# A share of the exponentials on VectorE, taken from the fourth chunk of each batch instead of the third

## The chip, the cores and the metric

The kernel runs on one core of a Trainium2 chip. The metric is device time in microseconds (us). Before the change the median of four runs is 318.1 us (317.76, 320.7, 318.44 and 317.64 us). A program with its instruction order fixed by hand runs on five engines that only meet at semaphores: TensorE (PE in the profile, with its weight loads as PEld), VectorE (DVE), ScalarE (ACT), GpSimd (POOL) and the engine that issues most DMAs (SP).

## The reference

Attention with a soft cap for 8 batches of 12 heads, 448 positions and head size 64, followed by a soft mixture of experts (8 experts with 4 slots each, so 32 slots):

```python
scores = scale * q @ k^T                  # scale = 1/8
scores = cap * tanh(scores / cap)         # cap = 30
attn   = softmax(scores);  x = attn @ v   # x: 3584 x 768
logits = x @ phi                          # 3584 x 32
d = softmax over the tokens; slots = d^T @ x
slot_out[e] = relu(slots[e] @ w1[e]) @ w2[e]
out = softmax over the slots (logits) @ slot_out      # 3584 x 768
```

Since the scores are capped at 30, the kernel takes their exponentials without subtracting the maximum. Every score goes through one tanh and one exponential.

## The kernel before, in words

**Tiles.** Two heads make a pair, and two pairs a quad, whose q and k are loaded, cast and transposed together. A pair has 7 score tiles of 128 x 448 (64 keys of each of its two heads on the partitions, 448 queries along the row). The 336 tiles of the 48 pairs are cut into 56 chunks of 6 tiles without regard to where a pair ends. One batch is 42 tiles, that is 7 chunks, so the work repeats every 7 chunks, and what is told below by "chunk number modulo 7" holds for every batch.

**One pass of the main loop** (line 523) handles one chunk j and puts work on the engines in this order:

- ScalarE: tanh of the two halves of chunk j (line 278, 1344 elements per partition each, from PSUM to the bf16 tile `ex`), then the exponentials of the chunk before, j-1, in place (line 282, 2688 elements).
- TensorE: half 0 of the attention output of one pair ("pv", lines 314 to 322: 14 matmuls whose weights are the exponentials), the scores of the first half of chunk j+1 (line 269, six matmuls of 64x64), half 1 of the same pair's output, and the scores of the second half of chunk j+1. The pair is the one whose last tile lies in chunk j-2; in the passes with j modulo 7 equal to 2 there is none.
- VectorE: after each half of a pair, the norm: the reciprocal of the row sums (line 328) and the product with it (line 329), which frees the PSUM tile for the next half.

Score tiles have two buffers of three tiles each (`psS`), so TensorE may fill one only when ScalarE's tanh of two groups ago has read it. All of the pairs' outputs share one PSUM tile (`psV`, line 312), and all small products (transposes, logits, slot sums) share another (`psT`). The chunks of exponentials have four buffers.

**The slots.** Between these steps stand five places in each pass, "0", "a", "b", "c" and "d" in that order, at which a list written by hand (`aux`, lines 426 to 493) inserts further jobs: casts of the raw q and k on VectorE, their transposes on TensorE, filling matmuls ("junk", line 506) and the logits and slot sums. "a" follows half 0 of the pair and its norm, "c" follows half 1 and its norm, "d" ends the pass. Each engine runs its own instructions strictly in this order.

**The shared exponentials.** From the second batch on, one tile per batch, the first of one chunk, doesn't get its exponential from ScalarE but from VectorE (`poly_exp`, lines 291 to 304): seven instructions on 448 elements per partition, in three parts. Part 0 (lines 294, 296 and 298) turns the scaled score into the bits of a float and splits them into exponent `xe` and mantissa `xm`. Part 1 (lines 300, 301) and part 2 (lines 303, 304) evaluate a polynomial, and line 304 writes the result over the tanh in `ex`. For that chunk ScalarE's instruction is 2240 elements long and not 2688 (line 285). The list `shared` (line 289) holds chunks 9, 16, 23, 30, 37, 44 and 51, those with number modulo 7 equal to 2. Part 0 stands in "c" of the chunk's own pass, part 1 in "a" and part 2 in "c" of the next one.

In pass j modulo 7 = 2 there are also the cast of q in "c" (line 226), the transposes of q (line 237) with their copy (line 239) and the logits of a quad (lines 355 and 360) in "d". The logits' PSUM tile is the one that the transposes of q need next, so TensorE goes on when VectorE has read the logits (`lg`, line 360). At the start of pass j modulo 7 = 4 ScalarE takes the exponentials of a batch's logits (`e_exp`, line 366) and GpSimd copies them four times over (`e_rep`, line 372).

After the loop come the last pairs, the two layers of the experts, and the output, which is written by SP's DMAs.

Of the kernel before, what the change touches and what calls it, by code (L numbers as in the profile page):

```python
# [32 lines left out]
def kernel(  # L33
# [20 lines left out]
    cap = float(cap)  # L54
# [6 lines left out]
    NCH = NTILE // CH  # L61
# [224 lines left out]

    shared = [j for j in range(NCH - 2) if j % 7 == 2 and j > 7] if cap < 80 else []

    def poly_exp(j, part):
        t, bits = exs[j][:, 0, :], 2.0 ** 23
# [135 lines left out]
    def at(j, slot, f, *a):  # L428
        if j < 0:
            j, slot = 0, "b"  # L430
        aux.setdefault((j, slot), []).append((f, a))
# [16 lines left out]
    for b in range(B):  # L448
        j = b * PER
# [30 lines left out]
            if b % 2:  # L480
                at(j + 14, "d", e_sums, b // 2)
    for j in shared:
        for dj, slot, part in ((0, "c", 0), (1, "a", 1), (1, "c", 2)):
            at(j + dj, slot, poly_exp, j, part)
    for n, job in enumerate(wjobs):
        at(1 + n * (NCH - 5) // len(wjobs), "b", *job)
# [244 lines left out]
    for n in range(B // 2 * NT):  # L731
        bb, c = divmod(n, NT)
# [61 lines left out]
```

## Time and profile before

The profiled execution took 317.76 us; its span, from the first to the last instruction, is 316.0 us, at a mean granted TensorE clock of 0.987.

| | 7 to 100 us | 100 to 200 us | 200 to 269 us | 269 to 284 us | 284 to 316 us |
|---|---|---|---|---|---|
| ScalarE busy, us | 92.9 | 100.0 | 69.0 | 3.2 | 13.3 |
| TensorE matmuls busy, us | 82.6 | 89.7 | 62.2 | 14.5 | 14.8 |
| VectorE busy, us | 58.9 | 67.5 | 43.5 | 4.7 | 16.1 |
| GpSimd busy, us | 38.8 | 39.3 | 22.3 | 2.4 | 0.6 |
| DMA, GB/s | 240 | 233 | 209 | 325 | 351 |

The first three columns are the main loop, the fourth the end of the attention and the experts, the fifth the output. In a row of a group, "busy" is the sum of its instructions and the number behind the last bar is the time for which the engine stood still just before them, with what ended it. In a row of the timeline the first number is the start and the second the duration, and "[1.18 <-DVE lg L360]" means that the engine had been idle for 1.18 us until that instruction released it. The recorded durations of ScalarE's instructions overlap: the next one is started before the end of the one before. Their ends are regular: a chunk's end comes 4.69 to 4.70 us after that of the chunk before, 4.31 to 4.33 us where the chunk is a shared one.

### The profile page before, as it was taken

To read this page: it belongs to the slowest core of one execution; us is meant where nothing else is said; L and a number is where in the kernel's file an instruction comes from. 1 tells how busy PE (TensorE), PEld (TensorE's weight loads), DVE (VectorE), ACT (ScalarE), POOL (GpSimd) and SP (SyncE) were. 2 spreads that over 40 slices of the span, in tenths; PEclk is the share of its full clock that TensorE was granted. 3 is DMA by queue.
4 is the path that set the end of the run, shared out by engine and by line. 5 is a ranking of instruction groups with operands and counts; after the bars stand their busy time and mean duration, and the time that the engine had idled before them with its cause. 6 is when DMAs were issued, how large, how long until landed. Compare 5 with 4: busy or idle time off the path is not lost.

```text
span 316.0 us, 8844 instructions
## 1 busy us (share of the span) xinstructions
PE 269.3 (85%) x3804; PEld 189.6 (60%) x3804; DVE 193.3 (61%) x473; ACT 281.3 (89%) x208; POOL 105.5 (33%) x134
## 2 busy tenths in 40 slices
PE   8899897889789989898989988997989898998720
PEld 6667575666566656675666656765666577743300
DVE  3736665766676668666767586658665654337740
ACT  4999999999999999999999999999999999135730
POOL 2554341523542453354245415452543030200000
PEclk9999999999999999999999999999999999999995
DMA  8899999799999989999999999999999807798997
GB/s 232 268 228 241 291 249 263 170 226 256 213 225 244 255 222 222 232 235 280 174 250 257 235 224 207 253 233 249 214 240 230 213 14 228 250 399 298 389 413 310
DMA packets 57478, 77.68 MB, mean 246 GB/s; under 512 B 3808, under 2 KB 53600, under 8 KB 57440
## 3 DMA queue, kind: packets, MB, share of 16 engines
q0 software_dynamic: 30480, 25.22, 52.1%
q1 hardware_dynamic: 26672, 51.68, 47.6%
q8 instruction: 29, 0.48, 0.6%
q10 hardware_dynamic: 288, 0.23, 0.2%
q14 instruction: 9, 0.07, 0.1%
HBM read 91.32 MB, written 18.87 MB: 349 GB/s over the span
## 4 chain that ended last, share of the span: by engine, by line
ACT 51%; PE 30%; DVE 10%; DMA 2%; issue 2%; SPq 0%; DVEq 0%; ACTq 0%
ACT ex L278 26%; ACT ex L282 24%; PE pv L318 9%; PE sc L269 5%; PE junk L506 3%; PE so_ps L676 2%; DVE xq L329 2%; PE hp L649 2%; DMA out_dram<-ob 2%; PE kps L237 1%; PE xps L344 1%; PE op L702 1%; PE boot L506 1%; PE slps L407 1%; DVE xp L301 1%
## 5 line engine op out<-in xcount | busy, mean ns | idle before, releaser
L278 ACT ACTIVATE ex<-sc 128x1344 bf16<-128x1344 f32 (+1 forms) x113 | 159.3, 1652 | 0.9 <-PE sc L269 0.8
L282 ACT ACTIVATE ex<-ex 128x2688 bf16<-128x2688 bf16 (+4 forms) x58 | 156.2, 2698 | 0.1
L318 PEld LDWEIGHTS <-ex 128*128 128x128 bf16 x1344 | 78.7, 97 | 22.1 <-DVE xq L329 17.4
L318 PE MATMUL pv<-vbd,ex 128*128 128x130 bf16 x1274 | 89.5, 220 | 2.4 <-ACT ex L282 0.7
L269 PE MATMUL sc<-qT,kT 64*64 64x448 bf16 x672 | 78.6, 359 | 3.0 <-ACT ex L278 2.5
L247 POOL CAST vbd<-vraw 64x896 bf16<-64x896 f32 x23 | 21.4, 929 | 108.4 <-PE pv L318 70.5
L329 DVE TENSOR_TENSOR xq<-pv,rec 128x256 bf16<-128x256 f32 x91 | 38.6, 424 | 3.2
L328 DVE RECIPROCAL rec<-pv 128x4 f32<-128x4 f32 x91 | 16.6, 182 | 36.3 <-PE pv L318 36.3
L269 PEld LDWEIGHTS <-kT 64*64 64x64 bf16 x672 | 25.8, 105 | 20.7 <-issue 2.6
L506 PEld LDWEIGHTS <-ones 128*128 128x128 bf16 x470 | 28.6, 101 | 11.8 <-DVE xq L329 8.2
L506 PE MATMUL junk<-ones 128*128 128x128 bf16 x433 | 31.4, 219 | 2.7 <-DVE xq L329 1.9
L372 POOL COPY e<-E 128x512 bf16<-128x512 bf16 x9 | 5.9, 653 | 78.2 <-ACT E L366 46.3
L239 DVE COPY kT<-kps 128x896 bf16<-128x896 bf16 x23 | 14.4, 625 | 24.0 <-PE kps L237 23.9
L109 POOL DMA_DIRECT2D w1b<-in_moe_w_dram x32 | 25.2, 792 | 0.2 <-issue 0.2
L248 POOL CAST vbd<-vraw 64x896 bf16<-64x896 f32 x23 | 24.0, 1042 | 1.3
L346 DVE COPY xT<-xps 128x512 bf16<-128x512 bf16 x47 | 19.6, 417 | 2.5 <-PE xps L344 2.4
L237 PE MATMUL qps<-ident,qbf 128*128 128x128 bf16 x161 | 12.8, 219 | 9.2 <-DVE lg L360 8.6
L344 PE MATMUL xps<-ident,xq 128*128 128x128 bf16 x188 | 18.1, 218 | 0.2 <-DVE zacc L383 0.2
L239 DVE COPY qT<-qps 128x896 bf16<-128x896 bf16 x23 | 14.2, 618 | 5.2 <-PE qps L237 5.2
L226 DVE CAST kbf<-kraw 128x896 bf16<-128x896 f32 x22 | 16.6, 756 | 1.2 <-DMA kraw<-in_k_dram 1.2
L237 PE MATMUL kps<-ident,kbf 128*128 128x128 bf16 x161 | 12.8, 219 | 4.2 <-DVE slacc L418 2.2
L237 PEld LDWEIGHTS <-qbf 128*128 128x128 bf16 x161 | 9.9, 97 | 10.5 <-issue 8.8
(113 smaller groups left out, 255.6 us busy)
## 6 DMA issues: line engine op xcount, KB each, us to landing
w1b<-in_moe_w_dram POOLq DMA_DIRECT2D x32, 384.0 KB, 9.4
vraw<-in_v_dram SPq DMA_DIRECT2D x23, 448.0 KB, 6.6
qraw<-in_q_dram SPq DMA_DIRECT2D x22, 448.0 KB, 7.8
kraw<-in_k_dram SPq DMA_DIRECT2D x22, 448.0 KB, 5.1
w2d<-in_moe_w_dram POOLq DMA_DIRECT2D x20, 384.0 KB, 9.2
w2t<-w2d SPq DMA_DIRECT2D x20, 384.0 KB, 5.3
out_dram<-ob SPq DMA_DIRECT2D x8, 768.0 KB, 7.8
w2b<-in_moe_w_dram POOLq DMA_DIRECT2D x12, 384.0 KB, 9.5
```

The costliest lines, as they stand in the source:

```text
L109: pool.dma_start(out=w1b[e][:, js, fs], in_=w1r[:, e, js, fs])
L237: pe.transpose(ps[:, c, :], src[:, c, :], ident)
L239: dve.tensor_copy(t, ps)
L247: pool.tensor_copy(t[0:HP, :, :, 0:DH], raw[0:HP])
L248: pool.tensor_copy(t[HP:P, :, :, DH + 1:VW - 1], raw[HP:P])
L269: pe.matmul(sc[cs, u, 0:S], qkT["k", Q][r, c, cs], qkT["q", Q][r, :, cs], start=True, stop=True)
L278: act.activation(exs[j][:, half * CS + u0:half * CS + u1, :], sc[:, u0:u1, 0:S], ACT.Tanh, scale=qk_scale / cap)
L282: act.activation(exs[j][:, u0:u1, :], exs[j][:, u0:u1, :], ACT.Exp, scale=cap)
L318: pe.matmul(pvs[pr, half][:, n, 0:VW], exs[j][:, u, GOFF[g]:GOFF[g] + P], vbds[Q % 2][:, h, c, :], start=(c == 0 and n == 0), stop=(c == N ...
L329: dve.tensor_tensor(xq[Q][:, 2 * half:2 * half + 2, h * P:(h + 1) * P] .rearrange("p g (i d) -> p g i d", i=2), pv[:, :, :, 0:DH], rec.to_ ...
L344: pe.transpose(ps[:, g, :], xq[Q][:, g, h * P:(h + 1) * P], ident)
L506: pe.matmul(junk if home is None else home, ones, ones, start=True, stop=True)
```

## The change

The shared chunk becomes the one with number modulo 7 equal to 3 (chunks 10, 17, 24, 31, 38, 45 and 52, again seven), and its three parts stand in "a", "c" and "d" of its own pass.

```diff
-    shared = [j for j in range(NCH - 2) if j % 7 == 2 and j > 7] if cap < 80 else []
+    shared = [j for j in range(NCH - 2) if j % 7 == 3 and j > 7] if cap < 80 else []
...
     for j in shared:
-        for dj, slot, part in ((0, "c", 0), (1, "a", 1), (1, "c", 2)):
+        for dj, slot, part in ((0, "a", 0), (0, "c", 1), (0, "d", 2)):
             at(j + dj, slot, poly_exp, j, part)
```

In VectorE's order this is what one batch's stretch looks like before and after (instructions by line, the same ones on both sides; passes by j modulo 7):

```
before: 226 q cast | 294 296 298 | 360 lg | 239 q copy | 328 329 norm, half 0 | 300 301 | 328 329 norm, half 1 | 303 304 | (pass 4) 328 329
after:  226 q cast | 360 lg | 239 q copy | 328 329 norm, half 0 | 294 296 298 | 328 329 norm, half 1 | 300 301 303 304 | (pass 4) 328 329
```

On ScalarE the short instruction of 2240 elements moves one pass later, behind line 366 instead of ahead of it. The order of TensorE, GpSimd and SP stays the same. A wait of TensorE on line 304 ahead of the weights of the shared tile goes away, since a norm behind line 304 is waited for anyhow.

## The prediction

> **What bounds the kernel.** I read the busy times by stretch first: ScalarE is busy for 261.9 of the 262 us from 7 to 269 us. The groups say the same from the other side (idle time is behind the last bar):
>
> ```profile
> L278 ACT ACTIVATE ex<-sc 128x1344 bf16<-128x1344 f32 (+1 forms) x113 | 159.3, 1652 | 0.9 <-PE sc L269 0.8
> L282 ACT ACTIVATE ex<-ex 128x2688 bf16<-128x2688 bf16 (+4 forms) x58 | 156.2, 2698 | 0.1
> ...
> L269 PE MATMUL sc<-qT,kT 64*64 64x448 bf16 x672 | 78.6, 359 | 3.0 <-ACT ex L278 2.5
> ```
>
> ScalarE's two large groups waited 1.0 us in all, at the very start. So within the main loop nothing can be gained: its length is ScalarE's own work, which the change leaves alone (seven tiles shared before and after). But the kernel doesn't end with ScalarE. The second view is the chain that ended last, in order of time:
>
> ```profile
> 210.48 1.19 ACT ex L278
> 211.67 0.04 issue
> 211.71 0.76 PE sc L269 x6
> ...
> 268.50 0.92 PE pvl L318 x16
> ```
>
> From 211.71 to 271.8 us no piece of this chain is ScalarE's: TensorE, with the VectorE steps it waits for, is a little behind ScalarE and stays so to the end. ScalarE's last exponential ends at 268.97 (267.50 + 1.47), TensorE's last pv matmuls start at about 270.1. What TensorE saves in the last batch the whole rest (experts, output) can start earlier by. In earlier batches it catches up anyway: the first scores issued in a batch's pass 2 (passes by j modulo 7) start 0.05 us after the tanh that frees their buffer ended (48.31, 80.99, 146.35, 211.71), 0.2 in two batches. In the last it doesn't: there they start 0.85 us late (245.19).
>
> So the third view is the timeline of the place that is changed, in the last batch:
>
> ```profile
> 247.50 0.36 PE L355 MATMUL lps<-phib,xT 128*128 128x32 bf16 x8
> 247.55 0.38 DVE L294 TENSOR_SCALAR xe<-ex 128x448 int32<-128x448 bf16 x1
> 247.97 0.39 DVE L296 TENSOR_SCALAR xm<-xe 128x448 int32<-128x448 int32 x1
> 248.40 0.40 DVE L298 TENSOR_SCALAR xe<-xe 128x448 int32<-128x448 int32 x1
> 248.71 0.28 DVE L360 TENSOR_TENSOR lg<-lps,lg 128x128 f32<-128x128 f32 x1
> 249.04 0.55 PE L237 MATMUL qps<-ident,qbf 128*128 128x128 bf16 x7 [1.18 <-DVE lg L360]
> ...
> 252.19 0.17 DVE L328 RECIPROCAL rec<-pv 128x4 f32<-128x4 f32 x1
> 252.40 0.42 DVE L329 TENSOR_TENSOR xq<-pv,rec 128x256 bf16<-128x256 f32 x1
> 252.50 0.61 POOL L372 COPY e<-E 128x512 bf16<-128x512 bf16 x1 [7.34 <-ACT E L366]
> 252.74 0.85 DVE L303 SCALAR_TENSOR_TENSOR xp<-xp,xm 128x448 f32<-128x448 f32 x1
> 252.88 1.40 PE L506 MATMUL junk<-ones 128*128 128x128 bf16 x18 [0.27 <-DVE xq L329]
> 253.62 0.62 DVE L304 SCALAR_TENSOR_TENSOR ex<-xp,xe 128x448 bf16<-128x448 f32 x1
> 254.33 0.96 PE L318 MATMUL pv<-vbd,ex 128*128 128x130 bf16 x14
> 255.33 0.18 DVE L328 RECIPROCAL rec<-pv 128x4 f32<-128x4 f32 x1 [1.08 <-PE pv L318]
> ```
>
> The logits' product ends at 247.86, but `lg` stands behind the three instructions of part 0 and starts at 248.71; the transposes of q stand still for 1.18 us until it is done. That wait is in every batch (1.18 to 1.30 us), and in the last one it lies on the chain.
>
> **The change, step by step, in the last batch.**
> *Part 0 leaves its place.* `lg` starts 0.04 us behind the product, at 247.90 in place of 248.71; the transposes start at 248.23 in place of 249.04. TensorE's stall falls from 1.18 to about 0.37 us: gain 0.81.
> *What could be late next on TensorE.* Half 0 of the pair would start at 248.78 (249.59 before); the exponentials it reads ended at 247.86. The next scores come at 249.6; their tanh ends at 249.04 (246.89 + 2.15). Neither stops it.
> *Part 0 at its new place.* Behind norm 0, whose product now starts at 249.84 (250.65 before), line 294 starts at 250.19 by the spacing that line 300 has now (0.35). Its new wait, for the tanh of its own chunk, costs nothing: that tanh ended at 249.04. Three instructions at the present spacing of 0.42 end at 251.44. Norm 1 is queued behind them, and TensorE's filling matmuls behind norm 1. Half 1 runs from 250.32 to 251.3, so norm 1 starts at about 251.35, as before just behind the work put ahead of it (part 1 takes 1.27, part 0 1.25 us). Its product ends at 251.98 and the matmuls start at 252.03: gain 0.85.
> *Parts 1 and 2 together.* They start at 251.90. L300 and L301 take 0.65 each by their spacing, L303 0.85 as now if GpSimd's copy meets it, L304 0.62: the end is at about 254.67. Queued behind is norm 0 of pass 4, whose pv ends at 253.48 + 0.96 + 0.04 = 254.48. It is held up by 0.1 to 0.2 us (255.33 before). But TensorE doesn't need it until its scores are done at 255.4 (256.2 before), and the product ends at 255.25. So the four instructions hide behind pv and the scores, with some 0.15 us to spare before TensorE feels them, and 0.8 more before the whole gain is gone.
> *ScalarE.* The exponentials ahead of line 366 are 2688 long in place of 2240: 2.33 in place of 1.96 us. E and one pair of tanh end 0.37 later, and the shared chunk one pass on gives it back. Scores that wait for these tanh are 1.89 and 2.31 us behind them now; 0.37 + 0.8 fits.
> *GpSimd and SP.* Their orders don't change. GpSimd's copy and the weight DMA issued behind it come 0.37 later, once per batch; GpSimd is a third busy. The raw loads of q and k hang on casts: that of q keeps its place, that of k behind norm 0 of the next pass moves by some tenths.
> *Does the gain last to the end?* TensorE 0.8 earlier must not run into ScalarE. Its margins are: scores at 259.27, tanh ended at 258.25 (1.02); pv at 262.65, exponentials at 261.75 (0.90); first pvl matmuls at 268.50, exponentials at 267.66 (0.84); the later ones 1.1. The smallest, 0.84, is just enough. Behind it come the experts and the output, a chain of TensorE and of DMAs that starts from it; no matmul of the second layer waited for a weight load.
> *Earlier batches.* TensorE gets to its scores up to 0.45 us earlier, waits there for ScalarE (lag 0.50 falls to 0.05), and ScalarE ends nothing earlier: 0.
>
> **Costs that no row shows.** Lines 300 to 304 have never stood in one run. From below, all clean, they take 2.5 us; from above, each at line 304's largest, 1.01, 4.05. I take 2.75, one of them slowed, since the copy (0.61) can meet one or two. With 4.05 the last batch's norm starts at about 255.9, and the gain of 0.8 becomes a loss of 0.5. The tail after 269 us may pass on from nothing to all of 0.8, as its last third is a chain of output DMAs that may run at their own rate; I take all, since each link of it starts from the one before.
>
> **A rule weighed.** Line 304 takes 0.62 us alone and 0.91 to 1.01 in the other six batches, where it starts up to 0.2 us behind the copy of line 372, and ends 0.47 or 0.48 us behind that copy's end; line 303 does the same in the last batch. The Trainium skill ("SBUF — State Buffer", section "Who interferes with whom") says that a VectorE instruction with two inputs in SBUF and a GpSimd instruction that reads SBUF exclude each other for a whole instruction, whichever started first. The trace agrees with that. By this rule it speaks against the change, which sets four such instructions in a row ahead of a norm; but one copy can then block only what starts within it, and the sum stays as above.
>
> **Sum.** 317.76 - 0.8 = 317.0 us against the profiled execution. The four runs' median is 318.1, 0.3 above it, drawn up by one at 320.7. I say 317.1.
>
> **Rivals.**
> *Nothing gained, 0.24.* The output's DMAs set the end, or norm 0 behind line 304 eats what `lg` gave. For it: output DMAs stand in the chain for up to 5.5 us in one piece, and VectorE has the same work in the same stretch. Against it: its idle time there (1.08 us before the norm at 255.33) is what would be used up. Time: 317.7, or 318.1 by the median.
> *Slower, 0.06.* VectorE's block of four, with norm 0 queued behind it, becomes the bound of the pass that follows. In the middle batches the block starts at about 153.17 (fourth of the seven) and would end, at 1.01 each, at 157.2; the norm that started at 156.05 would start at 157.1, and TensorE falls 1.1 us back. It decides from 0.97 us on, the smallest room that scores have before their tanh in most batches (0.67 in one). At 1.1 six batches cost 0.13 to 0.43 each, 1.1 together, and the last 0.5: 319.4. To pass 1% the norm would have to be 1.4 us late everywhere: 321.
> *The change doesn't do what it says, 0.04.* Line 360 could be held by something else at its new place; the stall of 1.18 us would stay: 317.8. More than 0.84 us can't come from it.
>
> **Chances.** Forecast 0.66, 317.0 give or take 0.4 for the spread of undisturbed runs. The range goes from 316.4 (all of 0.84 and a fast run) to 318.6 (no gain by the median, and 0.5 for the loss of the upper bound). A change of 1%, 3.2 us, is about what a measurement of this kernel can tell from none; faster by over 1% 0.02, within 1% 0.95, slower by over 1% 0.03.
>
> **What would show it.** In the new profile: the wait of the transposes of q for `lg` falls from 8.6 us in seven to about 2.5; ScalarE's groups still wait 1.0 us; TensorE's waits for line 278's tanh become more than six; from the shared pass of the last batch on every TensorE row is 0.8 earlier; the last exponential still ends at 269.0. Wrong would be: ScalarE idle before line 278 in every batch, or the output starting at 283.4 as before.

## The result

The changed kernel takes 317.49 us in the median of 43 runs (316.74 to 320.64), the kernel before 318.78 in 64 (317.3 to 321.54). The ratio is 0.9965, with a 95% interval from 0.9949 to 0.9981: faster by 0.35%, 0.6 to 1.6 us. The forecast was 0.8 us.

The groups of the profile after, in the same columns as before (busy and mean, then the idle time just before them and what ended it):

```profile
L278 ACT ACTIVATE ex<-sc 128x1344 bf16<-128x1344 f32 (+1 forms) x113 | 162.4, 1693 | 1.1 <-PE sc L269 0.8
L282 ACT ACTIVATE ex<-ex 128x2688 bf16<-128x2688 bf16 (+4 forms) x58 | 159.3, 2779 | 0.1
...
L269 PE MATMUL sc<-qT,kT 64*64 64x448 bf16 x672 | 78.6, 358 | 8.0 <-ACT ex L278 7.8
...
L237 PE MATMUL qps<-ident,qbf 128*128 128x128 bf16 x161 | 12.8, 219 | 3.5 <-DVE lg L360 2.7
```

ScalarE waits as little as before (1.2 us against 1.0). TensorE's time before the scores (line 269) grew from 3.0 to 8.0 us, nearly all of it waits for ScalarE's tanh (7.8 us in 19 waits, 2.5 in 6 before): TensorE now reaches its scores early and finds their buffer still in use. Its wait for the logits ahead of the transposes of q fell from 8.6 to 2.7 us.

The timeline of the last batch after the change:

```profile
248.55 0.29 DVE L360 TENSOR_TENSOR lg<-lps,lg 128x128 f32<-128x128 f32 x1 [0.27 <-PE lps L355]
...
248.89 0.55 PE L237 MATMUL qps<-ident,qbf 128*128 128x128 bf16 x7 [0.38 <-DVE lg L360]
...
252.55 0.62 DVE L300 SCALAR_TENSOR_TENSOR xp<-xm 128x448 f32<-128x448 f32 x1
...
253.20 0.63 DVE L301 SCALAR_TENSOR_TENSOR xp<-xp,xm 128x448 f32<-128x448 f32 x1
...
253.58 0.72 POOL L372 COPY e<-E 128x512 bf16<-128x512 bf16 x1 [7.77 <-ACT E L366]
...
253.86 0.91 DVE L303 SCALAR_TENSOR_TENSOR xp<-xp,xm 128x448 f32<-128x448 f32 x1
...
254.81 0.62 DVE L304 SCALAR_TENSOR_TENSOR ex<-xp,xe 128x448 bf16<-128x448 f32 x1
...
255.35 0.17 DVE L328 RECIPROCAL rec<-pv 128x4 f32<-128x4 f32 x1
255.56 0.43 DVE L329 TENSOR_TENSOR xq<-pv,rec 128x256 bf16<-128x256 f32 x1
...
256.05 0.97 PE L318 MATMUL pv<-vbd,ex 128*128 128x130 bf16 x14
```

The stall of 1.18 us is one of 0.38. Yet these rows stand at about the same times as before the change, not 0.8 earlier. That is because this execution began later. Its first tanh starts at 7.01 in place of 6.59, as the first k and q arrived later, and its fourth exponential ends another 0.28 later: ScalarE's whole row is 0.70 us late, by what happens ahead of any shared chunk. So the absolute times of two profiles can't be set against each other here, and I take a measure that leaves the start out: **the gap behind ScalarE**, from the end of its last exponential (line 282) to the start of the experts' first matmul (line 649). It was 273.61 - 268.97 = 4.64 us before the change and is 273.59 - 269.67 = 3.92 after it: 0.72 us less. The rows before (`pvl` is the output of the last pair, in a PSUM tile of its own):

```profile
256.13 0.97 PE L318 MATMUL pv<-vbd,ex 128*128 128x130 bf16 x14
...
266.28 2.69 ACT L282 ACTIVATE ex<-ex 128x1344 bf16<-128x1344 bf16 x3
...
268.34 1.08 PE L318 MATMUL pvl<-vbd,ex 128*128 128x130 bf16 x16
...
269.48 0.85 PE L318 MATMUL pvl<-vbd,ex 128*128 128x130 bf16 x12
...
273.61 1.48 PE L649 MATMUL hp<-w1b,slT 128*32 128x512 bf16 x24
```

And after:

```profile
266.20 3.47 ACT L282 ACTIVATE ex<-ex 128x1344 bf16<-128x1344 bf16 x3
...
268.25 1.14 PE L318 MATMUL pvl<-vbd,ex 128*128 128x130 bf16 x16
...
269.46 0.85 PE L318 MATMUL pvl<-vbd,ex 128*128 128x130 bf16 x12
...
273.59 1.48 PE L649 MATMUL hp<-w1b,slT 128*32 128x512 bf16 x24
```

The 0.5 us between the two spans (316.0 and 315.5) are +0.70 at the start, -0.72 in the gap and -0.48 behind it (42.39 and 41.91 us), where the output's transfers happened to wait less; in the kernels below that last stretch lies anywhere between 41.88 and 42.52.

About one execution in four (26 of 89 of the kernel before whose spans are on record, 8 of 44 of the one after) is some 2.7 us longer; ratios over ten runs move by some tenths of a per cent with how many of these they catch. The two profiles below that are of such executions (all but the last batch changed, and the stall put back in all seven) begin late: their fourth exponential ends at 31.6 or 31.7 us, in the others between 28.2 and 29.0. It isn't the loads: ScalarE's first cast of k starts at 4.91 and 4.84 us there, at 4.83 in the profile after. TensorE is slow at first: in the former of the two the first twelve score matmuls take 2.45 us, in the profile after 1.32. So the table below gives, besides the ratio, the middle span of the runs without them (those up to 317.1 us; of the four kernels that take longer than before, marked *, the middle of all runs).

| kernel | ratio to before, 95% interval | gap, us | middle span, us |
|---|---|---|---|
| before | 1 | 4.64 | 316.2 |
| after | 0.9965 (0.9949 to 0.9981) | 3.92 | 315.5 |
| only the last batch changed, first time | 0.9964 (0.9934 to 0.9994) | 4.68 | 315.6 |
| only the last batch changed, again | 0.9968 (0.9939 to 0.9997) | 3.91 | 315.75 |
| all but the last batch changed | 0.9994 (0.9963 to 1.0025) | 4.62 | 316.15 |
| after, tile of the third chunk | 1.014 (1.0097 to 1.0182) | 4.68 | 321.95* |
| after, stall put back in all seven | 1.007 (1.0036 to 1.0104) | 4.69 | 319.3* |
| after, stall put back in the last | 0.9962 (0.9939 to 0.9984) | 4.63 | 316.15 |
| after, stall put back in the first six | 1.005 (1.0023 to 1.0077) | 4.69 | 318.1* |
| before, less filling | 0.9984 (0.9956 to 1.0012) | 4.07 | 315.4 |
| after, less filling | 0.9981 (0.9953 to 1.001) | 3.92 | 315.6 |
| after, two tiles per batch | 1.0061 (1.0031 to 1.009) | 4.68 | 318.4* |
| after, first batch shared too | 0.9989 (0.9963 to 1.0016) | 4.41 | 315.9 |

### The profile page after: what moved, and what is told of

The parts are those of the page before. It is cut to its first block, busy times and chain, and to the rows that moved or that the text cites. A ratio compares the mean times of both kernels' runs of the same rounds, so it can differ in the third digit from the quotient of the medians.

```text
span 315.5 us, 8844 instructions
## 1 busy us (share of the span) xinstructions
PE 269.8 (86%) x3804; PEld 191.4 (61%) x3804; DVE 194.0 (62%) x473; ACT 281.3 (89%) x208; POOL 106.4 (34%) x134
## 4 chain that ended last, share of the span: by engine, by line
ACT 64%; PE 22%; DVE 5%; issue 3%; DMA 2%; DVEq 0%; SPq 0%; ACTq 0%
ACT ex L278 32%; ACT ex L282 31%; PE pv L318 5%; PE sc L269 4%; PE junk L506 2%; PE so_ps L676 2%; PE hp L649 2%; DMA out_dram<-ob 2%; PE op L702 1%; PE boot L506 1%; DVE xq L329 1%; PE xps L344 1%; PE kps L237 1%; DMA out_dram<-obh 1%; ACT ob L754 1%
## 5 line engine op out<-in xcount | busy, mean ns | idle before, releaser
L278 ACT ACTIVATE ex<-sc 128x1344 bf16<-128x1344 f32 (+1 forms) x113 | 162.4, 1693 | 1.1 <-PE sc L269 0.8
L282 ACT ACTIVATE ex<-ex 128x2688 bf16<-128x2688 bf16 (+4 forms) x58 | 159.3, 2779 | 0.1
L318 PE MATMUL pv<-vbd,ex 128*128 128x130 bf16 x1274 | 88.6, 220 | 2.6 <-ACT ex L282 0.7
L269 PEld LDWEIGHTS <-kT 64*64 64x64 bf16 x672 | 27.3, 105 | 25.2 <-issue 7.5
L372 POOL COPY e<-E 128x512 bf16<-128x512 bf16 x9 | 7.2, 797 | 81.0 <-ACT E L366 49.0
L113 POOL DMA_DIRECT2D w2d<-in_moe_w_dram x20 | 15.4, 777 | 0.0
```

The lines of the kernel that those rows point to most:

```text
L269: pe.matmul(sc[cs, u, 0:S], qkT["k", Q][r, c, cs], qkT["q", Q][r, :, cs], start=True, stop=True)
L278: act.activation(exs[j][:, half * CS + u0:half * CS + u1, :], sc[:, u0:u1, 0:S], ACT.Tanh, scale=qk_scale / cap)
L282: act.activation(exs[j][:, u0:u1, :], exs[j][:, u0:u1, :], ACT.Exp, scale=cap)
L318: pe.matmul(pvs[pr, half][:, n, 0:VW], exs[j][:, u, GOFF[g]:GOFF[g] + P], vbds[Q % 2][:, h, c, :], start=(c == 0 and n == 0), stop=(c == N ...
```

## The experiments

**Which batches give the gain.** Two kernels that split the change: in one only the last batch is as after the change, in the other all but the last.

```diff
-    shared = [j for j in range(NCH - 2) if j % 7 == 3 and j > 7] if cap < 80 else []
+    shared = [j for j in range(NCH - 2) if j % 7 == (3 if j > 45 else 2) and j > 7] if cap < 80 else []
...
-        for dj, slot, part in ((0, "a", 0), (0, "c", 1), (0, "d", 2)):
+        for dj, slot, part in (((0, "a", 0), (0, "c", 1), (0, "d", 2)) if j % 7 == 3 else
+                               ((0, "c", 0), (1, "a", 1), (1, "c", 2))):
```

The second has `(2 if j > 45 else 3)`.

> The six earlier batches share as before the change (chunks 9 to 44, old places), the last one as after it (chunk 52, new places). Measure beside the time: the gap from the end of ScalarE's last exponential (line 282) to the start of the experts' first matmul (line 649), 4.64 us before the change and 3.92 after it. Theory, only the last batch counts, since TensorE enters it late and carries its delay into the tail: the whole gain, ratio 0.9975, gap 3.9. Rival, each batch gives a seventh: ratio 0.9995, gap 4.5.

> The opposite: chunks 10 to 45 shared as after the change, the last batch (chunk 51) as before it. Theory: six stalls of 1.2 us fall to 0.4 and nothing is gained, since TensorE then waits for ScalarE's tanh; ratio 1.000, gap 4.6, ScalarE's groups still wait 1 us in all. Rival, each batch gives a part: ratio 0.997, gap 4.0.

With only the last batch changed the ratio was 0.9964, as with the whole change. Its profile, though, is of an execution in which the granted clock fell twice (0.81 and 0.85 in the stretches of 5 us from 115 us on, 0.71 and 0.95 from 215 us on). There ScalarE lost 1.3 us: two chunks ended 5.63 and 5.48 us behind the one before, in place of 4.89. So its gap of 4.68 says nothing. With all but the last batch changed, the ratio was 0.9994 and the gap 4.62: nothing gained, though ScalarE was waited for there just as after the change (TensorE 7.4 us before line 269, 7.0 of it for line 278). ScalarE's two groups waited 3.5 us there and not the 1 expected; it is one of the executions that began late. The kernel with the last batch alone was run again for a readable profile:

> The kernel of the first experiment once more (only the last batch as after the change), for a profile in which the clock does not fall. Theory, only the last batch counts: gap behind ScalarE 3.9 (4.64 before), the transposes of q wait about 1.2 us six times and 0.4 once, ratio 0.9965 to 0.9975. Rival, every batch gives a part: gap 4.5.

Its group of scores:

```profile
L269 PE MATMUL sc<-qT,kT 64*64 64x448 bf16 x672 | 78.6, 359 | 3.1 <-ACT ex L278 2.8
```

The gap is 3.91, the ratio 0.9968. TensorE's idle time before the scores is 3.1 us, as before the change, and the transposes of q wait 7.6 us in all: six stalls of 1.2 us stand where they stood, and the whole gain is there without them. The last batch, which gives a seventh of the gain by the rival, gives all of it.

**Is it TensorE's delay, or something in VectorE's work?** A kernel before the change in which nothing of the exponentials is touched: of the 18 filling matmuls at the end of pass 52, whose product nothing uses, 8 are left out. And the same in the kernel after the change.

```diff
-    for j, slot, n in ((NCH - 6, "d", 8), (NCH - 4, "d", 8), (NCH - 2, "d", 12)):
+    for j, slot, n in ((NCH - 6, "d", 8), (NCH - 2, "d", 12)):
```

> The kernel before the change, without the 8 filling matmuls at the end of pass 52 (of the 18 there; their product is used by nothing). Nothing of the shared exponentials is touched. Theory, TensorE's delay in the last batch goes straight into the tail: 8 x 0.077 = 0.62 us less delay, gap behind ScalarE 4.0 in place of 4.64, ratio 0.998. Rival one, the gain of the change had to do with VectorE's work and not with TensorE's delay: ratio 1.000, gap 4.6. Rival two, the fillings hold the clock up: the granted clock falls behind pass 52, ratio above 1.000.

> The same 8 filling matmuls left out of the kernel after the change. Theory, the change has used up TensorE's delay and ScalarE bounds the last batch again (its first exponential of the last chunk ended 0.06 us before the matmuls that read it): almost nothing more, gap 3.6 to 3.9, ratio 0.996 as after the change. Rival, TensorE was still the bound: gap 3.3, ratio 0.9945.

Before the change the gap fell by 0.57 us to 4.07, for 0.62 us of matmuls left out. After the change it didn't fall at all: 3.92 and 3.92. (The ratio there, 0.9981, is above the 0.996 expected; its interval takes in 0.9965, and the middle span of 315.6 us is within 0.1 of the kernel after.) So TensorE's delay in the last batch is worth its length until ScalarE is reached, and the change has reached it. Here are the rows that say so, of the kernel after with less filling:

```profile
265.80 3.45 ACT L282 ACTIVATE ex<-ex 128x1344 bf16<-128x1344 bf16 x3
...
267.86 1.12 PE L318 MATMUL pvl<-vbd,ex 128*128 128x130 bf16 x16
...
269.04 0.85 PE L318 MATMUL pvl<-vbd,ex 128*128 128x130 bf16 x12
```

ScalarE's last three exponentials end at 269.25, and the last twelve pv matmuls start at 269.04, 0.21 us ahead of that end. In the kernel after, with all its filling, it is 269.46 against 269.67: 0.21 as well. Before the change they started 0.51 behind the end (269.48 against 268.97). With less filling TensorE has reached the point at which it takes each exponential as it comes, and so had the kernel after; the sixteen ahead of them take 1.12 and 1.14 us, against 1.08 before.

**Is the stall the cause?** After the change, three more VectorE instructions per batch where part 0 stood before. They read a piece of the transposed k, in the forms of lines 294 to 298, and nothing uses their result. (The lines behind 291 have numbers higher by 4 to 6 in these kernels.)

```diff
     def poly_exp(j, part):
-        t, bits = exs[j][:, 0, :], 2.0 ** 23
-        if part == 0:
+        if part == 3:
+            t = qkT["k", 3 * (j // 7) + 2].rearrange("p c k -> p (c k)")[:, 0:S]
+        else:
+            t = exs[j][:, 0, :]
+        bits = 2.0 ** 23
+        if part in (0, 3):
...
             at(j + dj, slot, poly_exp, j, part)
+        at(j - 1, "c", poly_exp, j, 3)
```

> As after the change, with three more VectorE instructions per batch where part 0 stood before: the same forms as lines 294 to 298, reading part of the transposed k and leaving a result that nothing uses. They put the logits' stall back and nothing else (VectorE has 1.25 us more to do per batch, in a place where it had idle time). Theory, the stall of 1.18 us ahead of the transposes of q is the whole cause: ratio 1.000, gap 4.6, the transposes wait 8 us or more in seven. Rival, the gain came from the order of norms and polynomial: gap 3.9, ratio 0.9975.

The stall came back (8.6 us in seven waits) and with it the gap (4.69). But the time didn't return to 1.000, it went to 1.007: the stall did more here than in the kernel before the change. To tell where, I put it back in the last batch alone and in the first six alone (`if j > 45` or `if j <= 45` ahead of the added line).

> As after the change, with the three idle VectorE instructions of the stall put back in the last batch alone. Theory, a stall in the last batch costs its own length and no more: gap 4.6 to 4.8, ScalarE loses nothing, ratio 0.999 to 1.000. Rival, it was these three that made the run with all seven slow in some other way: ratio well above 1.000.

> The same three instructions in the six earlier batches alone. Theory, formed from the run with all seven: the stall of 0.8 us and VectorE's block of four, with a norm behind it, add up to more than TensorE's room of about 1 us before ScalarE's tanh; ScalarE idles some 0.7 us in every second batch and the last batch starts later: ratio 1.002 to 1.005, gap 3.9 to 4.2. Rival, the stalls of the earlier batches are made good there, as in the kernel before the change: ratio 0.9965 as after the change, gap 3.9.

In the last batch the stall costs its length and no more: gap 4.63, with 1.0 us of waits of ScalarE in all, as before the change, and a middle span of 316.15 us against 316.2. (That no run of ten began late makes the ratio 0.9962 and not the 0.999 expected.) In the first six it costs far more than before the change: 1.005. The timeline of the fourth batch there:

```profile
118.79 0.55 PE L237 MATMUL qps<-ident,qbf 128*128 128x128 bf16 x7 [1.33 <-DVE lg L364]
...
124.71 0.62 DVE L308 SCALAR_TENSOR_TENSOR ex<-xp,xe 128x448 bf16<-128x448 f32 x1
...
125.25 0.18 DVE L332 RECIPROCAL rec<-pv 128x4 f32<-128x4 f32 x1
...
125.47 0.42 DVE L333 TENSOR_TENSOR xq<-pv,rec 128x256 bf16<-128x256 f32 x1
...
125.94 0.97 PE L322 MATMUL pv<-vbd,ex 128*128 128x130 bf16 x14 [0.69 <-DVE xq L333]
```

The stall of 1.33 us pushes VectorE's block of four back, the norm stands behind it, and TensorE stands still a second time, 0.69 us, for that norm. The chunks of ScalarE that follow end 4.88, 5.01 and 4.75 us apart in place of 4.69: it has lost 0.6 us. Two batches on it is 5.07, 5.02 and 4.75, and the batch in between loses 0.1. I had expected the gap to stay at 3.9 to 4.2; it is 4.69, as TensorE enters the last batch late: its first scores of pass 2 start 23.0 us ahead of the end of the last exponential, and 23.8 in the profile after.

**Could the tile have stayed where it was?** VectorE's order as after the change, instruction by instruction, with the tile of the third chunk.

```diff
-... if j % 7 == 3 and j > 7] if cap < 80 else []
+... if j % 7 == 2 and j > 7] if cap < 80 else []
...
-        for dj, slot, part in ((0, "a", 0), (0, "c", 1), (0, "d", 2)):
+        for dj, slot, part in ((1, "a", 0), (1, "c", 1), (1, "d", 2)):
```

> VectorE's order as after the change, instruction by instruction, but the tile is again that of the third chunk (parts in a, c and d of the pass behind). Theory: the logits' stall is gone as after the change, but the pv matmuls of the next pass read the tile, so the weights of the shared tile wait for line 304 (it ends some 0.6 us behind the first weights that are ready) and pv's last third comes late: about two thirds of the gain are lost, gap 4.4, ratio 0.999. Rival, the order on VectorE is all and the chunk is indifferent: gap 3.9, ratio 0.9975.

It was slower by 1.4%, far from either expectation. The timeline of the fifth batch, and the busy times in stretches of the third (columns: busy time and number of instructions of TensorE's matmuls and weight loads, VectorE, ScalarE and GpSimd, then the granted clock, the DMA share and GB/s):

```profile
161.88 0.63 DVE L304 SCALAR_TENSOR_TENSOR ex<-xp,xe 128x448 bf16<-128x448 f32 x1
...
162.57 0.40 PE L318 MATMUL pv<-vbd,ex 128*128 128x130 bf16 x4 [1.28 <-DVE ex L304]
```

```profile
85.00:90.00 5.00, 4.33 (x62) 2.82 (x59) 3.93 (x11) 5.00 (x4) 0.26 (x1) 1.00 1.08 217
90.00:95.00 5.00, 3.66 (x35) 2.27 (x36) 4.07 (x8) 5.00 (x5) 1.55 (x2) 0.78 1.19 244
95.00:100.00 5.00, 4.55 (x58) 3.57 (x57) 1.25 (x4) 4.00 (x4) 3.19 (x4) 0.50 0.65 146
100.00:105.00 5.00, 4.93 (x48) 3.32 (x47) 2.88 (x8) 2.56 (x3) 0.92 (x2) 0.70 1.01 193
```

The pv matmuls that read the tile wait 8.2 us in seven stalls for line 304. I had worked with the last batch, where 18 filling matmuls precede them; elsewhere there are 10, so they are ready 0.6 us sooner and wait longer. In the stretch shown the clock falls to 0.50 behind such a stall, and ScalarE idles 3.4 us. Here the chunk is anything but indifferent: the fourth chunk's tile is read a pass later, and no weight load or matmul waits for it in the profile after (before the change the weight loads waited 0.7 us for line 304, in three stops).

**Two versions meant to be faster still.** With ScalarE bounding the loop again, more of its work was moved: a second tile per batch, or one in the first batch too.

```diff
+    shared += [j for j in range(NCH - 2) if j % 7 == 1 and j > 7] if cap < 80 else []
...
-        for dj, slot, part in ((0, "a", 0), (0, "c", 1), (0, "d", 2)):
+        for dj, slot, part in (((0, "a", 0), (0, "c", 1), (0, "d", 2)) if j % 7 == 3 else
+                               ((0, "a", 0), (0, "d", 1), (1, "a", 2))):
```

> As after the change, and a second tile per batch on VectorE: the first tile of the chunks with number modulo 7 equal to 1 (8 to 50), part 0 behind norm 0 of its pass, part 1 at that pass's end, part 2 in the next pass, which has no norms. Theory, ScalarE bounds the loop after the change and TensorE has some 1.3 us per batch to wait for it: 7 x 0.37 = 2.6 us less, ratio 0.988. Rival, as in the two runs that put the stall back or kept the third chunk, norms that come late behind VectorE's work cost more than ScalarE saves: ratio 1.000 or more, ScalarE idle before line 278.

Slower, 1.0061. The ends of ScalarE's chunks 39 to 45 come 5.07, 5.02, 4.74, 4.70, 4.32, 4.89 and 4.52 us apart, 33.26 together; after the change seven take 4.52 + 6 x 4.69 = 32.66. (Line 366 adds 0.20 us to one chunk per batch. After the change that is the shared one, 4.32 + 0.20; before it, it was the chunk behind the shared one, which came 4.89 us behind it and not 4.69 as the others.) The chunk of 4.32 shows the 0.37 saved, the first two what TensorE's lateness takes: it stands still 3.8 us in seven waits for a norm.

The other version takes `and j > 7` out of the list `shared`, which adds chunk 3.

> As after the change, and chunk 3 of the first batch shared too. Theory, ScalarE's chain sets the time: 0.37 us less than after the change, ratio 0.995. Rival, in the first batch TensorE is behind anyway (scores 0.26 us ahead of their tanh) and the earlier end of ScalarE's instruction only turns into a wait: ratio 0.9965 as after the change, or worse.

Its ratio is 0.9989, between before and after, and none of it a gain over after. The second expectation came true: what ScalarE saved in chunk 3 was lost in chunk 4, whose exponentials ended 5.15 us behind those of chunk 3 in place of 4.69. A norm stood behind VectorE's block of four, TensorE stood still 0.82 us for it (until 27.81 us), and ScalarE 0.34 us for TensorE (until 28.59). From the first tanh to the end of the last exponential this execution took 262.36 us, no less than that of the kernel before with 262.38 (the profile after, with its slower start, has 262.66). That the gap was 4.41 has another reason: at 237.45 us VectorE's cast of q had waited 0.53 us for the load of q, and TensorE stood still 0.50 us for the cast. No version beat the kernel after the change.

## Why the prediction was right

*ScalarE bounds the loop, and earlier batches give nothing.* Right, and shown: 0.9994 with six batches changed. There TensorE's first scores of pass 3 (by j modulo 7) start 0.05 us behind the tanh in the profile after, where they started 0.49 to 0.90 behind it before: the forecast trade of one wait for another.

*TensorE's delay in the last batch goes into the tail.* Right, and shown from two sides: the change in the last batch alone gives the whole gain, and leaving out fillings gives 0.57 us for 0.62.

*The stall falls by 0.81 us.* It fell from 1.18 to 0.38, 0.80. Set against ScalarE, the scores that follow came 0.86 us sooner (0.43 us behind the tanh that frees their buffer, 1.29 before).

*The four instructions hide.* Right, with a term a little undersized. I took 2.75 us for the block; it took 2.88 (252.55 to 255.43). Line 303 met GpSimd's copy at 0.91 and not 0.85, and I had left out the spacing behind it. The norm behind the block started at 255.35, 0.68 us sooner than before against ScalarE's end, not 0.78, and its product came at 255.99, when the scores ended at 256.02: the room of 0.15 us was used to the last, but no more. The pv matmuls that follow start 0.78 us sooner against ScalarE's end (256.13 before, 256.05 after).

*The smallest margin, 0.84 us.* It was smaller, and that is why the gap fell by 0.72 and not by 0.8. I had the start of the first pvl matmuls from the chain, 268.50, where a piece begins when the one before it has ended; by the timeline they start at 268.34. The third of the sixteen is the first that reads one of ScalarE's last three exponentials. Before the change it started at 268.45, 0.79 us behind the end of that exponential (267.66); after it, at 268.42, 0.05 behind (268.37). The first of the sixteen still comes 0.79 us sooner against ScalarE's end, the last twelve 0.72: there TensorE has reached ScalarE, and less filling gains nothing more.

*Two readings of rows were off.* The wait ahead of the transposes was 1.17 to 1.42 us in the seven batches before the change, not 1.18 to 1.30, and line 304 started up to 0.49 us behind the copy, not 0.2. Neither stands in the sum.

*The measured gain is 1.1 us with 0.6 to 1.6 as its interval; the gap explains 0.7.* The spans without late starts differ by 0.7 too. What the ratio has beyond that lies within its interval, and nothing here shows a cause for it. Two things on record could add to it. Fewer executions after the change began late, which may be chance. And a mean granted clock below 0.979 stands in 24 of 143 runs of the kernels that have the stall in the six earlier batches (before, last batch alone, stall put back in seven or six, before with less filling), but in 2 of 102 of those that don't (after, all but the last, stall put back in the last, after with less filling, two tiles, first batch too). Before the change, runs without a late start took 316.8 us in the mean at such a clock (7 runs), the others 316.2. That the stall lowers the clock is suggested by this, not shown.

*My sign of failure was badly chosen.* I wrote that the output starting at 283.4 as before would prove me wrong. It started at 283.37. The start of this execution was 0.70 us later, and absolute times can't tell a gain hidden by that from no gain. The last exponential, too, ended at 269.67 and not at 269.0.

*The slower rival* didn't come, but its mechanism, norms behind VectorE's block that make TensorE late for ScalarE, was one step away: with the stall put back in six batches it cost 0.5%, with a second tile 0.6%, both against the kernel before. I had put its start at 0.97 us of lateness; with the stall back ScalarE loses in every second batch.

## What to carry to other kernels

Where one engine is busy without a gap, look for who is late when it ends. In this kernel a wait of TensorE cost nothing in the middle, as long as its room ahead of ScalarE took it up, and its full length in the last batch. Compare such profiles by the distance from an event of the bounding engine, not by absolute times, since a late start of 0.7 us hides a gain of 0.7. Two moves that each look free can need each other: the later tile with the logits' stall put back (by three instructions more on VectorE), or the earlier logits without the later tile, made this kernel slower than it had been.

## What the runs showed of the hardware

Short stops of TensorE were followed by falls of the granted clock, but not always. In the kernel with the tile of the third chunk a stop of 1.28 us, in the third batch, was followed by 0.78, 0.50 and 0.70 in three stretches of 5 us from 90 us on, and one of 1.31 us, in the second, went with 0.86 and 0.80 from 55 us on. Four more stops of 1.27 or 1.28 us, and the last one of 0.54, left the clock at 1.00. Of the six runs of that kernel five had a mean clock of 0.966 to 0.972, where the kernel after is at 0.979 to 0.987. In the first run with the last batch alone the falls at 115 and 215 us went with stops of 1.46 and 1.37 us ahead of the transposes of q, and fourteen pv matmuls behind the first one took 1.72 us in place of 0.96. In the profile before, a stop of 1.42 us left the clock at 1.00. What decides it isn't shown.

GpSimd's copy of line 372, 0.61 us in the median before, took 0.87 after. It now starts while VectorE is in line 303 (in the last batch in line 301) and ends some 0.47 us behind that instruction, and the VectorE instruction that starts during the copy ends some 0.47 us behind the copy. In the fifth batch line 303 ran from 155.32 to 155.95, the copy from 155.54 to 156.42, and line 304 from 155.98 to 156.89, 0.91 us where it takes 0.62 alone. In these rows each of the two delays the other, depending on which came first.
